# Reordering the opening of an FFT-attention and ELU-MLP kernel: what is asked for first, who prepares the bias and M3, and in which order M2 is made

## The chip, the cores and the metric

One core of one Trainium2 chip. The metric is the device time of one execution in microseconds (us), the median of several runs. The engines are named as in the profile: PE (TensorE; PEld is its weight load), DVE (VectorE), ACT (ScalarE), POOL (GpSimd) and SP (SyncE, which here only issues DMAs).

## The reference, cut to what matters

```python
def _attn_ref(x, w_r, w_i, b_r, b_i):            # x: (8, 3008, 256)
    X = np.fft.rfft(x, axis=1)
    Xr, Xi = X.real, X.imag
    Yr = Xr @ w_r - Xi @ w_i + b_r
    Yi = Xr @ w_i + Xi @ w_r + b_i
    lam = 0.01                                   # soft threshold
    Yr = np.sign(Yr) * np.maximum(np.abs(Yr) - lam, 0.0)
    Yi = np.sign(Yi) * np.maximum(np.abs(Yi) - lam, 0.0)
    return np.fft.irfft(Yr + 1j * Yi, n=3008, axis=1)

def _moe_ref(x, w_in, w_out):                    # x: (24064, 256), d_ff 2048
    h = x @ w_in
    g = np.where(h > 0.0, h, np.exp(np.minimum(h, 0.0)) - 1.0)
    return g @ w_out
```

## The kernel before, in words

The transform of length 3008 = 47 x 64 is done as two steps of matrix products, forward and back. Each of the 8 batches passes five kinds of unit:

- A (6 units a batch, `unit_A`): a product of x with the matrix M1; the result goes from PSUM to the tile A and from there to DRAM (DA). `load_Z` reads it back in another order as Z, in four quarters for batch 0.
- X (8 units, `unit_X`): products of Z with M2, whose 32 slots are used four by four in a unit; two units share a quarter of Z. The result is copied to XT. For batch 0 PSUM has two buffers for A and X (pool `pre2`), so a unit waits for the copy of the one two before it.
- M (12 units): the product with w_r and w_i, bias, and the soft threshold, giving Y. In batch 0 it is `first_M`; there every second unit has the bias added by PE, as a product of a tile of ones (`busy`) with `bias_p`, and its clip is on ACT, while for the other units DVE adds `bias_bc` and POOL clips and subtracts.
- B (6 units, `unit_B`): products of Y with M3, to DRAM (DB) and back as Bs (`load_Bs`).
- Y (8 units): products of Bs with M4, giving yT, the input of the MLP.

The MLP is a long loop over blocks of 512 rows, in which the units of the later batches are woven by a planner; it starts when batch 0 has come through all five. Everything ahead of the loop is the opening. It runs in the order in which the code is written: each engine works through its own instructions in that order and waits where it needs another's result. PE gets filler products (`idle_pe(n)`: n products of `busy` with itself, used by nothing) where it would stand idle.

In the opening the matrices M1 to M4 are computed on the chip from index patterns that POOL makes (`iota`). M2 is made in four groups of slots (g = 0 to 3), each in the passes

- `points(g)` (DVE, three instructions): the phase's integer part, and a sign row `st`;
- `phases(g)` (DVE, or ACT with `on_act`): to turns, in `v2`;
- `wraps(g)` (DVE, two instructions): less the nearest integer;
- `sizes(g)` (ACT): the absolute value, in `a2`; `signs(g)` (DVE): back to a signed phase of the cosine;
- `sines(g, 0)` and `sines(g, 1)` (ACT): the two sines, into M2; `slot0` (DVE, four narrow instructions) mends slot 0.

M3 needs v3 (a product of two index rows), w3 (v3 less its nearest integer, two instructions) and a3 (ACT, the absolute value of w3), then two sines on ACT (`M3f[0]`) and two products on DVE (`M3f[1]`). In the kernel before, DVE makes v3 (L672) behind M2's last signs and w3 (L725, L726) behind it, and a3 stands on ACT (L732) behind the first X copies.

The bias for PE is split into three bf16 parts whose sum is the f32 bias. Before, it comes in three f32 rows (partitions 0, 32 and 64 of `brow`, six DMAs on SP at the very start), is cast on ACT (L727), and DVE takes the rest, casts it, and takes the rest again (L728, L733 to L736).

The DMAs that matter are on two queues, in the order in which they are issued. SP: the bias rows, A's six writes, the weights w_r and w_i (L631, L632), Z's quarters (these wait for all of A's writes), `bias_bc`, the first quarter of w_in, and later B's writes and Bs. POOL: x of batch 0 in six pieces (`first_x`, between the iotas), and, behind a `gate` (L706, a copy that reads one column of Z), x of batch 1 and w_out. POOL also makes `wcat_r` and `wcat_s`, the bf16 weights of M (L633 to L636), and issuing a DMA takes its time.

## Time and profile before

| | before |
| --- | --- |
| runs | 881.12 us median of 3 (880.57 to 881.66) |
| the profiled execution | 879.84 us |
| its span (first to last instruction) | 877.9 us |
| busy share of the span | PE 98%, PEld 80%, ACT 83%, DVE 75%, POOL 74% |
| granted clock of PE | 0.998 |
| x of batch 0: DMAs on POOL's queue | 6 of 512 KB, 6.0 us to landing (median) |
| weights w_r, w_i: DMAs on SP's queue | 2 of 256 KB |

How to read it: times in the profile count from the span's start. The opening is the first 57 us or so. A line of the timeline gives start, length, engine, source line, operation, what is written and read, and in brackets how long the engine stood idle before it and what ended that. A line of the chain of waits gives start, length and what the end of the program hung on at that time. A group (line, engine, operation, tiles, shapes) ends in its count, its busy time, the mean length of one in ns, and its engine's idle time just ahead of it. SPq and POOLq are the DMA issues of SP and POOL.

### The profile page before, as it was taken

Reading aid. Unit: us, or ns where it says so; the run is one execution under the profiler, and the core shown is the slowest. Engines: PE = TensorE matmul, PEld = TensorE weight load, DVE = VectorE, ACT = ScalarE, POOL = GpSimd, SP = SyncE. Lnnn points to the kernel's source line nnn. Section 1 sums busy time; section 2 is a strip of 40 time slices with the busy share of each in tenths; the row PEclk is TensorE's granted clock in tenths of the full one; section 3 lists DMA queues with packets and bytes.
Section 4 is the critical chain, followed back from the end, with each engine's and each line's share of the span. In section 5 each row is a group of like instructions: output and inputs, shape, how many; then the busy total and the mean of one; then the engine's idle time right before and its main releaser. Section 6 shows DMA issues by size and latency. Waiting matters only on the chain.

```text
span 877.9 us, 20548 instructions
## 1 busy us (share of the span) xinstructions
PE 863.4 (98%) x7817; PEld 702.8 (80%) x7817; DVE 656.6 (75%) x1066; ACT 725.9 (83%) x1217; POOL 651.9 (74%) x981
## 2 busy tenths in 40 slices
PE   8889999999999999999999999999999999999997
PEld 3448887888888888888889888898888988888886
DVE  8767886678777787677776777767776788777775
ACT  6668998899888997899978999789987888786664
POOL 6707995689667887698866888668886699756664
PEclk9999999999999999999999999999999999999999
DMA  8995346743484444642564344553444023421111
GB/s 265 354 263 137 113 115 179 203 140 85 127 252 151 124 118 118 180 141 81 151 174 130 125 130 115 154 169 94 137 118 134 26 67 82 129 77 34 43 32 49
DMA packets 106382, 116.68 MB, mean 133 GB/s; under 512 B 10886, under 2 KB 96012, under 8 KB 103404
## 3 DMA queue, kind: packets, MB, share of 16 engines
q1 hardware_dynamic: 100124, 87.85, 35.6%
q0 software_dynamic: 6016, 27.40, 9.9%
q8 instruction: 61, 1.00, 0.5%
q14 instruction: 37, 0.30, 0.1%
q10 hardware_dynamic: 144, 0.13, 0.0%
HBM read 55.32 MB, written 49.81 MB: 120 GB/s over the span
## 4 chain that ended last, share of the span: by engine, by line
PE 86%; POOL 6%; DVE 4%; DMA 1%; issue 1%; ACT 1%; POOLq 0%; DVEq 0%; SPq 0%
PE ps_o L913 36%; PE hps L861 35%; PE mps L262 5%; PE xps L197 2%; PE aps L163 2%; PE yps L397 2%; POOL Et L883 2%; PE bps L356 1%; POOL Y L293 1%; PE mps L214 1%; DVE gT L895 1%; DVE yb L279 1%; POOL yb L288 1%; PE bps L347 1%; POOL clip L289 1%
## 5 line engine op out<-in xcount | busy, mean ns | idle before, releaser
L895 DVE SCALAR_TENSOR_TENSOR gT<-Et,hps 128x512 fp32r<-128x512 f32 x752 | 493.4, 684 | 161.1 <-POOL Et L883 160.2
L913 PE MATMUL ps_o<-w_out_r,gT 128*128 128x256 f32 x3008 | 473.0, 299 | 0.1
L883 POOL TENSOR_SCALAR Et<-Et 128x512 f32<-128x512 f32 x576 | 350.2, 615 | 164.6 <-ACT Et L878 163.4
L861 PE MATMUL hps<-yT,w_in_s 128*128 128x64 bf16 (+9 forms) x2800 | 441.1, 282 | 1.7 <-DVE gT L895 0.6
L913 PEld LDWEIGHTS ps_o<-w_out_r,gT 128*128 128x128 f32 x3008 | 399.4, 188 | 46.3 <-ACT osb L928 0.4
L878 ACT ACTIVATE Et<-hps 128x512 f32<-128x512 f32 x584 | 343.4, 604 | 96.8 <-PE hps L861 93.4
L861 PEld LDWEIGHTS <-w_in_s 128*128 128x128 bf16 x2800 | 163.8, 98 | 57.6 <-issue 13.7
L875 ACT ACTIVATE Et<-hps 128x512 f32<-128x512 f32 x168 | 99.6, 593 | 18.8 <-PE hps L861 18.0
L876 ACT ACTIVATE Et<-Et 128x512 f32<-128x512 f32 x168 | 106.2, 632 | 5.3
L293 POOL TENSOR_TENSOR Y<-yb,clip 128x512 bf16<-128x512 f32 x84 | 108.6, 1293 | 0.3
L288 POOL TENSOR_TENSOR yb<-yb,bias_d 128x256 f32<-128x256 f32 x68 | 49.8, 732 | 29.8 <-DVE yb L279 29.6
L289 POOL TENSOR_SCALAR clip<-yb 128x512 f32<-128x512 f32 x84 | 51.6, 614 | 13.2 <-DVE yb L275 7.0
L246 POOL TENSOR_TENSOR Xd<-XT 128x256 bf16<-128x256 bf16 x84 | 56.5, 673 | 0.0
L130 ACT CAST A<-aps 128x1024 bf16<-128x1024 f32 x45 | 45.3, 1009 | 6.9 <-PE aps L163 6.8
L130 ACT CAST XT<-xps 128x768 bf16<-128x768 f32 x61 | 48.5, 794 | 3.0 <-PE xps L197 3.0
L130 ACT CAST yT<-yps 128x752 bf16<-128x752 f32 x63 | 49.2, 781 | 2.1 <-PE yps L397 2.1
L262 PE MATMUL mps<-wsum,XT 128*128 128x256 bf16 x336 | 50.4, 273 | 0.0
L279 DVE TENSOR_TENSOR yb<-mps,Kb 128x512 f32<-128x512 f32 x68 | 47.0, 692 | 2.5
L278 DVE TENSOR_TENSOR Kb<-mps,bias_bc 128x256 f32<-128x256 f32 x68 | 28.7, 422 | 23.3 <-PE mps L262 23.3
L163 PE MATMUL aps<-xt,M 128*128 128x512 f32 x96 | 38.0, 477 | 2.1 <-DMA xt<-in_x_dram 0.9
L397 PEld LDWEIGHTS <-Bs 96*128 96x128 bf16 x512 | 27.8, 98 | 13.3 <-DMA Bs<-DB 1.8
L370 ACT CAST Bz<-bps 128x1024 bf16<-128x1024 f32 x36 | 36.3, 1007 | 0.0
(124 smaller groups left out, 503.8 us busy)
## 6 DMA issues: line engine op xcount, KB each, us to landing
xt<-in_x_dram POOLq DMA_DIRECT2D x21, 1024.0 KB, 5.6
out_dram<-osb SPq DMA_DIRECT2D x158, 128.0 KB
Bs<-DB SPq DMA_DIRECT2D x32, 384.0 KB
DA<-A SPq DMA_DIRECT2D x21, 512.0 KB
DB<-Bz SPq DMA_DIRECT2D x20, 512.0 KB
Z<-DA SPq DMA_DIRECT2D x26, 384.0 KB
Yt<-Y SPq DMA_DIRECT2D x144, 64.0 KB
xt<-in_x_dram POOLq DMA_DIRECT2D x6, 512.0 KB, 6.0
```

What stands on the lines that cost most here:

```text
L130: nc.scalar.copy(dst, src)
L262: nc.tensor.matmul(dst, lhsT=lhs(dt), rhs=rhs(dt), start=dt == 0, stop=dt == 1)
L288: nc.gpsimd.tensor_tensor(yb[:, D : 2 * D], yb[:, D : 2 * D], bias_d[:], ALU.add)
L289: nc.gpsimd.tensor_scalar(clips[0][:], yb[:], LAM, -LAM, ALU.min, ALU.max)
L293: nc.gpsimd.tensor_tensor(Y_, two(yb), two(clips[0]), ALU.subtract)
L861: nc.tensor.matmul(hps[s][:, a:z], lhsT=w_in_s[:, dt, ft * P : ft * P + P], rhs=yT_of[b][:, dt, t0 + a - c0 : t0 + z - c0], start=(dt == 0 ...
L875: nc.scalar.activation(e, h, AF.Relu, scale=-1.0)
L876: nc.scalar.activation(e, e, AF.Exp, scale=-1.0)
L878: nc.scalar.activation(e, h, AF.Exp)
L883: nc.gpsimd.tensor_scalar(e, e, 1.0, 0.0, ALU.min, ALU.max)
L895: nc.vector.scalar_tensor_tensor(g_of[self.i][:, p], self.E[:, p], -1.0, self.h[p], ALU.add, ALU.max)
L913: nc.tensor.matmul(po[q][:, i_ % 2, :], lhsT=gT[:, s, i_ * P : i_ * P + P], rhs=w_out_r[:, ft, :], start=(ft == 0 and i_ % 2 == 0), stop=( ...
```

## The change

What is asked for first: w_r and w_i are the first two DMAs of SP, ahead of everything; the bias comes in two DMAs of 4 x 64 in place of six of 1 x 256. On POOL's queue `first_x(0)` moves ahead of the first iota. Fillers at the start: 7 in place of 9.

The bias: POOL splits it, on 8 partitions x 64 elements (five narrow instructions), into `bpart`; DVE clears `bias_p`, and three DMAs on SP, behind Z's, put the parts into rows 0 to 2. DVE's and ACT's six instructions on the bias go.

M3's phases: v3 and w3 go from DVE to POOL (four instructions with the scaled index row n2s), w3's last one behind the first request for x of batch 1; a3 moves on ACT from behind unit 1 to behind unit 6 of X.

The weights of M: `wcat_r` goes from POOL to ACT (two copies, among the sines), `wcat_s` stays on POOL, behind w3's first instruction.

M2's passes: DVE makes group 1's phases at once, groups 2 and 3 have theirs on ACT, and the sines of groups 0 and 1 stand next to each other; `slot0` and groups 2 and 3 follow. Fillers ahead of X: 31 in place of 40.

Copies: unit 5 of A uses two PSUM buffers of the M units' pool, and its halves are copied by DVE and ACT at once (`both`). X's units are copied by ACT and DVE in turn (before, DVE had units 1, 4 and 7). The gate reads Z's first quarter (slot 0), not its second (slot 8).

```diff
-    def unit_A(b, u, alone=False, on_dve=False, ahead=False):
+    def unit_A(b, u, alone=False, on_dve=False, ahead=False, both=False):
...
-        ps = unit_ps("aps", alone or ahead)
+        if both:
+            two = [pre1.tile([P, 512], F32, name="aps", tag="mps1")[:] for _ in range(2)]
+        else:
+            ps = unit_ps("aps", alone or ahead)
+            two = [ps[:, j, :] for j in range(2)]
...
+            if both:
+                for j in range(2):
+                    evac(dst[:, 512 * j : 512 * j + 512], two[j], j == 0)
+            else:
+                evac(dst, ps[:].rearrange("p a b -> p (a b)"), on_dve)
...
-    brow, rest = (wk3.tile([P, 2 * D], F32, name="yb", tag="yb") for _ in range(2))
-    nc.vector.memset(brow[:], 0.0)
-    for o, bv in ((0, b_r), (D, b_i)):
-        for k in range(3):
-            nc.sync.dma_start(
-                brow[32 * k : 32 * k + 1, o : o + D],
-                bass.AP(tensor=bv.tensor, offset=bv.offset, ap=[[0, 1], [1, D]]),
-            )
-    idle_pe(9)
+    brow_t = wk3.tile([P, 2 * D], F32, name="yb", tag="yb")
+    bpart_t = wk3.tile([P, 4 * D], BF16, name="yb", tag="yb")
+    brow = brow_t[0:8, 0 : 2 * N2].rearrange("p (k d) -> p k d", k=2)
+    bpart = bpart_t[0:8, 0 : 3 * N2].rearrange("p (k d) -> p k d", k=3)
+    w_r_f, w_i_f = (wk3.tile([P, 2, D], F32, name=nm, tag="Y") for nm in ("w_r_f", "w_i_f"))
+    nc.sync.dma_start(w_r_f[:], w_r.rearrange("(c p) e -> p c e", p=P))
+    nc.sync.dma_start(w_i_f[:], w_i.rearrange("(c p) e -> p c e", p=P))
+    for o, bv in ((0, b_r), (4, b_i)):
+        nc.sync.dma_start(
+            brow[o : o + 4, 0], bass.AP(tensor=bv.tensor, offset=bv.offset, ap=[[N2, 4], [1, N2]])
+        )
+    idle_pe(7)
...
+        first_x(0)
         pcol = iota("pcol", [P, 1], [[0, 1]], cm=1)
...
-        first_x(0)
         first_x(1)
...
+        nc.vector.memset(bias_p, 0.0)
...
+        for k in range(3):
+            pool.tensor_copy(bpart[:, k], brow[:, k % 2])
+            if k < 2:
+                pool.tensor_tensor(brow[:, 1 - k], brow[:, k], bpart[:, k], ALU.subtract)
...
-            unit_A(0, u, alone=True)
+            unit_A(0, u, alone=True, both=u == 5)
...
         points(1)
-        phases(1, True)
+        phases(1)
+        wraps(1)
+        sizes(0)
         points(2)
-        sizes(0)
         fA(4)
-        wraps(1)
-        signs(0)
+        sizes(1)
         fA(5)
-        nc.sync.dma_start(w_r_f[:], w_r.rearrange("(c p) e -> p c e", p=P))
-        nc.sync.dma_start(w_i_f[:], w_i.rearrange("(c p) e -> p c e", p=P))
-        pool.tensor_copy(wcat_r[:, :, 0:D], w_r_f[:])
-        pool.tensor_copy(wcat_r[:, :, D : 2 * D], w_i_f[:])
-        pool.tensor_scalar(wcat_s[:, :, 0:D], w_i_f[:], -1.0, None, ALU.mult)
-        pool.tensor_copy(wcat_s[:, :, D : 2 * D], w_r_f[:])
         for g in range(4):
             load_Z(0, 8 * g, 8 * g + 8)
+        for k in range(3):
+            nc.sync.dma_start(
+                bias_p[k : k + 1, :].rearrange("p (a d) -> p a d", a=8), bpart[:, k]
+            )
...
+        phases(2, True)
         sines(0, 0)
-        sizes(1)
-        phases(2, True)
+        sines(1, 0)
+        signs(0)
+        sines(0, 1)
...
+        full = [P, NV, N2]
+        n2s = row("n2s", [P, N2])
+        pool.tensor_scalar(n2s[:], n2row, 1.0 / S, None, ALU.mult)
+        pool.tensor_tensor(
+            v3[:], n2s[:].unsqueeze(1).to_broadcast(full), k3[:].unsqueeze(2).to_broadcast(full),
+            ALU.mult,
+        )
+        pool.tensor_scalar(w3[:], v3[:], CMAGIC, -CMAGIC, ALU.add, ALU.add)
+        pool.tensor_scalar(wcat_s[:, :, 0:D], w_i_f[:], -1.0, None, ALU.mult)
+        pool.tensor_copy(wcat_s[:, :, D : 2 * D], w_r_f[:])
+        signs(1)
+        nc.scalar.copy(wcat_r[:, :, 0:D], w_r_f[:])
+        nc.scalar.copy(wcat_r[:, :, D : 2 * D], w_i_f[:])
+        sines(1, 1)
+        slot0()
+        wraps(2)
+        sizes(2)
         points(3)
-        phases(3)
-        wraps(2)
-        signs(1)
-        sines(0, 1)
-        sines(1, 0)
-        sizes(2)
-        sines(1, 1)
+        phases(3, True)
+        signs(2)
+        sines(2, 0)
+        sines(2, 1)
         wraps(3)
-        signs(2)
-        slot0()
-        sines(2, 0)
         sizes(3)
-        sines(2, 1)
         signs(3)
...
-        dve.scalar_tensor_tensor(
-            v3[:], n2row.unsqueeze(1).to_broadcast(full), 1.0 / S, k3b, ALU.mult, ALU.mult
-        )
-        idle_pe(40)
+        idle_pe(31)
...
-    gate(Z_of[0][:, 8, 0:1])
-    for ci in range(3):
-        load_x(1, ci)
+    gate(Z_of[0][:, 0, 0:1])
+    load_x(1, 0)
+    nc.gpsimd.tensor_tensor(w3[:], v3[:], w3[:], ALU.subtract)
+    load_x(1, 1)
+    load_x(1, 2)
...
-    nc.vector.tensor_scalar(w3[:], v3[:], CMAGIC, -CMAGIC, ALU.add, ALU.add)
-    nc.vector.tensor_tensor(w3[:], v3[:], w3[:], ALU.subtract)
-    nc.scalar.copy(bias_p, brow[:])
-    nc.vector.tensor_tensor(rest[:], brow[:], bias_p, ALU.subtract)
     for u in range(8):
-        unit_X(0, u, alone=True, on_dve=u in (1, 4, 7))
-        if u == 1:
+        unit_X(0, u, alone=True, on_dve=bool(u % 2))
+        if u == 6:
             nc.scalar.activation(a3[:], w3[:], AF.Abs)
-            nc.vector.tensor_copy(bias_p[32:64], rest[32:64])
-            nc.vector.tensor_copy(bias_p[64:P], rest[64:P])
-            nc.vector.tensor_tensor(rest[64:P], rest[64:P], bias_p[64:P], ALU.subtract)
-            nc.vector.tensor_copy(bias_p[64:P], rest[64:P])
```

More of the change, by code (lines that the diff above doesn't have):

```diff
@@ L160, in unit_A @@
         dav = DA_of[b].rearrange("j p d -> p j d")
-        ps = unit_ps("aps", alone or ahead)
+        if both:
[3 more added lines that the diff above has]
+            two = [ps[:, j, :] for j in range(2)]
         for j in range(2):
             nc.tensor.matmul(
-                ps[:, j, :], lhsT=M1[:],
+                two[j], lhsT=M1[:],
                 rhs=xt[:, 4 * uu + 2 * j : 4 * uu + 2 * j + 2, :], start=True, stop=True,
@@ L167, in done @@
         def done():
-            evac(
-                A[:, 4 * uu : 4 * uu + 4, :].rearrange("p n d -> p (n d)"),
-                ps[:].rearrange("p a b -> p (a b)"), on_dve,
-            )
+            dst = A[:, 4 * uu : 4 * uu + 4, :].rearrange("p n d -> p (n d)")
+            if both:
[3 more added lines that the diff above has]
+                evac(dst, ps[:].rearrange("p a b -> p (a b)"), on_dve)
             j0 = 8 * ci
@@ L462 @@
         w3, a3 = (wk2.tile([P, NV, N2], F32, name="A", tag="A") for _ in range(2))
-        w_r_f, w_i_f = (wk3.tile([P, 2, D], F32, name=nm, tag="Y") for nm in ("w_r_f", "w_i_f"))
         nc.scalar.activation(dume[:], busy[:, 0:1], AF.Sin, bias=0.0, scale=0.0)
+        first_x(0)
         pcol = iota("pcol", [P, 1], [[0, 1]], cm=1)
@@ L667 @@
         sines(3, 1)
-        full = [P, NV, N2]
-        k3b = k3[:].unsqueeze(2).to_broadcast(full)
-        dve.scalar_tensor_tensor(
-            v3[:], n2row.unsqueeze(1).to_broadcast(full), 1.0 / S, k3b, ALU.mult, ALU.mult
-        )
-        idle_pe(40)
+        idle_pe(31)
     gatep = ctx.enter_context(tc.tile_pool(name="gatep", bufs=2))
```

## The prediction

> **What bounds the kernel now.** Read first: the span and the busy shares, then busy time by stretches of the opening (columns: length, busy time and instructions of PE, PEld, DVE, ACT, POOL, granted clock, DMA share, GB/s).
>
> ```profile
> span 877.9 us, 20548 instructions
> PE 863.4 (98%) x7817; PEld 702.8 (80%) x7817; DVE 656.6 (75%) x1066; ACT 725.9 (83%) x1217; POOL 651.9 (74%) x981
> 13.40:22.90 9.50, 9.35 (x42) 4.12 (x42) 9.15 (x23) 8.01 (x16) 4.28 (x5) 1.00 0.91 262
> 22.90:31.04 8.14, 5.69 (x74) 3.55 (x74) 7.31 (x11) 5.50 (x8) 6.16 (x8) 1.00 1.05 326
> 31.04:47.30 16.26, 16.26 (x106) 6.96 (x106) 9.78 (x14) 11.69 (x16) 10.81 (x12) 1.00 1.29 353
> ```
>
> TensorE is busy to 98% of the span, so a microsecond that the opening saves ahead of the first M unit goes through to the end, if what follows comes along. From 31.04 to 47.30 PE never rests. In the 9.5 us before 22.9 most of PE's work is fillers. So the part that can shrink is what lies ahead of 31.04. The chain of waits there (start, length, what):
>
> ```profile
> 20.96 0.52 DVE a L581
> 21.47 0.88 DVE Bz L672
> 22.38 0.86 DVE A L725
> ...
> 24.13 1.10 DVE yb L728
> 25.23 0.88 DVE XT L128
> ...
> 30.02 0.97 DVE XT L128
> ...
> 48.73 3.03 DMA DB<-A
> ```
>
> VectorE carries it: after its share of M2 it computes M3's phases (L672, L725, L726) and the split of the bias (L728), and only then empties X's unit 1, at 25.23. Its last X copy ends at 30.99; call this T. The other leg of the opening is data, seen in the timeline and the DMA issues:
>
> ```profile
> 0.83 0.14 POOL L451 IOTA pcol<- 128x1 f32 x1 [0.40 <-POOLq L1137]
> 1.48 1.36 POOL L119 DMA_DIRECT2D xt<-in_x_dram  x2
> 6.15 0.71 POOL L119 DMA_DIRECT2D xt<-in_x_dram  x1
> 7.62 8.04 SPq L175 DMA_DIRECT2D DA<-A  x6
> xt<-in_x_dram POOLq DMA_DIRECT2D x1, 512.0 KB, 7.2
> 13.38 1.90 ACT L130 CAST A<-aps 128x1024 bf16<-128x1024 f32 x2
> 18.78 1.27 SPq L186 DMA_DIRECT2D Z<-DA  x3
> 22.91 0.37 PEld L197 LDWEIGHTS <-Z 96*128 96x128 bf16 x8 [0.61 <-DMA Z<-DA]
> 24.44 0.37 PEld L197 LDWEIGHTS <-Z 96*128 96x128 bf16 x8 [0.56 <-DMA Z<-DA]
> ```
>
> The last x piece is asked for at 6.15 and lands 7.2 later, 13.35. Its A unit is copied by 15.28 (13.38 + 1.90), Z is asked for at 18.78, and Z's quarters land at 22.9 and 24.4, so by the same step of 1.53 (my estimate for the last two) at 26.0 and 27.5.
>
> **The change part by part.**
>
> *Weights and x asked for first.* x's first request moves ahead of three iotas and two memsets, 0.65 earlier (1.48 to 0.83). One request takes half of 1.36, so the iotas end where they ended, about when VectorE is free to use them. Ahead of x, SP asks for 0.52 MB of weights as soon as the engines start (about when pcol does, 0.83); it had asked for them behind A's writes. What this costs x is read from the queues (packets, MB), up to 3 (one row, x alone) and from 9 to 12, and from the rates of three stretches:
>
> ```profile
> q0 software_dynamic: 5, 0.02, 3.7%
> ...
> q0 software_dynamic: 289, 1.05, 105.3%
> q1 hardware_dynamic: 38, 0.02, 2.7%
> 3.00:4.00 1.00, 1.00 (x4) 0.32 (x3) 0.89 (x5) 0.23 (x1) 1.00 (x5) 1.00 0.83 157
> 4.00:5.00 1.00, 0.96 (x4) 0.23 (x2) 0.79 (x6) 0.03 (x1) 0.93 (x5) 1.00 1.09 389
> 18.00:19.00 1.00, 1.00 (x7) 0.43 (x5) 0.96 (x4) 0.99 (x3) 0.00 (x0) 1.00 0.96 326
> ```
>
> A's writes (q1) were asked for from 7.6 on and got 38 packets in these 3 us beside x's 289: requests are served nearly in the order in which they come. So the weights go before most of x. At 326 GB/s they take 1.6 us; they can start about 1 us before x did (x had 5 packets by 3, its first full microsecond is 3 to 4), and the slow first microsecond (157 against 389 GB/s) falls to them. x's last piece lands 0.5 later, 13.85, by my estimate. Bounds: 0.65 earlier (weights wholly in the idle start) and 0.95 later (1.6 less 0.65). The two bias requests behind them are 1 KB each, and one request a bias replaces three.
>
> [...]
>
> *Unit 5's copy split over both engines.* ACT did units 4 and 5 in one row of 1.90. Now unit 5 is two halves at once; a 512-wide ACT copy is the 602 ns row below. 13.85 + 0.70 (matmuls) + 0.6 = 15.15: 0.1 earlier than 15.28 (bounds -1.25 and +0.35, those of x).
>
> *No weights behind A's last write.* From the last write's issue (right behind the copy, about 15.3; SP's six end at 15.66) to Z's request pass 3.4 us, with the weights' packets in the same queue; the write in the chain's row, DB<-A, took 3.03. I take 0.6 off (bounds 0 and 0.9). Z's request is then 0.7 earlier, 18.1; Z's quarters land at 22.2, 23.7, 25.3, 26.8.
>
> *M2's passes.* The last sine was:
>
> ```profile
> 21.50 0.52 ACT L591 ACTIVATE M<-a 96x384 bf16<-96x384 f32 x1 [0.93 <-DVE a L581]
> L727 ACT CAST spare<-yb 128x512 bf16<-128x512 f32 x1 | 0.6, 602 | 0.0
> L130 ACT CAST XT<-xps 128x768 bf16<-128x768 f32 x5 | 4.0, 797 | 3.0 <-PE xps L197 3.0
> ```
>
> It ended at 22.0. The work is the same, but ACT gains two copies of the weights (2 x 0.60) among it, and phase 1 goes from ACT to VectorE while phase 3 goes the other way. ACT waited 0.93 for VectorE before this sine, so part of the copies hides in such waits. I take 22.9 for ACT's last sine and 22.4 for VectorE's last sign; bounds 22.0 (all hidden) and 23.9 (both copies and 0.7 of contention on the path). ACT's copies of X queue behind that sine.
>
> *X.* VectorE now has nothing between its signs and X's copies, and copies alternate. Two PSUM buffers take turns; a unit's matmuls take 0.5, a copy 0.8 on ACT and 0.95 on VectorE (30.02's row: 0.97):
>
> ```profile
> 22.91 0.52 PE L197 MATMUL xps<-M,Z 96*128 96x96 bf16 x8
> 19.39 3.40 PE L412 MATMUL ips<-spare 128*128 128x512 bf16 x15
> ```
>
> ACT copies unit 0 from 22.95 to 23.75; unit 2's matmuls run 23.8 to 24.3, its copy to 25.15; unit 4 waits for Z at 25.3, copy 25.9 to 26.7; unit 6 waits for Z at 26.8, copy 27.4 to 28.2. VectorE: unit 1 23.35 to 24.3, unit 3 24.9 to 25.85, unit 5 26.45 to 27.4, unit 7 (matmuls 27.45 to 27.95) 28.0 to 28.95. T = 28.95 against 30.99: **2.0 earlier**. The fillers ahead of X, 31 instead of 40 at 0.22 (3.40 by 15), end at 14.55 + 6.9 = 21.4 and stay off the path; 40 would end at 23.4 and cost 1.2.
>
> *M3 and the bias.* VectorE loses L672, L725, L726 and L728 to L736, about 6 us in all; GpSimd gets M3's phases and the bias parts. ACT's Abs, which stood after unit 1, now follows unit 6, and the two sines of M3 behind it. The rows that tell what waits:
>
> ```profile
> 31.04 0.96 DVE L747 SCALAR_TENSOR_TENSOR M3f<-M3f,sg 128x768 bf16<-128x768 bf16 x1
> 32.69 1.25 POOL L328 TENSOR_SCALAR clip<-yb 128x512 f32<-128x512 f32 x1 [3.63 <-DVE yb L224]
> 34.02 1.27 POOL L329 TENSOR_TENSOR Y<-yb,clip 128x512 bf16<-128x512 f32 x1
> 35.68 0.61 PE L347 MATMUL bps<-Y,M3f 64*128 64x256 bf16 x8
> ```
>
> L747 needs M3's first sine: 28.2 + 0.75 (Abs) + 0.75 = 29.7, 0.75 after unit 7's copy where it began 0.05 after it. The first bias add behind it on VectorE, then GpSimd's clip and subtraction (34.02 + 1.27 = 35.29, T + 4.3), come 0.55 later against T, at T + 4.85; PE's first B unit came at T + 4.7. Queued behind Abs on ACT, which now waits for GpSimd's w3, are both sines and the clips of every second M unit. So **0.15 is lost again** (bounds 0 and 1).
>
> *GpSimd.* It sat idle for 5.14 us up to 19.33 (first row). Now it has the bias parts (five narrow operations, about 2 us by estimate; the 512-wide L633 took 0.75), v3 and w3 (768 wide), wcat_s, the gate, one x request, w3's subtraction, then the other requests. Prices:
>
> ```profile
> 19.33 0.75 POOL L633 CAST wcat_r<-w_r_f 128x512 bf16<-128x512 f32 x1 [5.14 <-DMA w_r_f<-in_w_r_dram]
> L329 POOL TENSOR_TENSOR Y<-yb,clip 128x512 bf16<-128x512 f32 x5 | 6.3, 1269 | 0.4
> L289 POOL TENSOR_SCALAR clip<-yb 128x512 f32<-128x512 f32 x84 | 51.6, 614 | 13.2 <-DVE yb L275 7.0
> L635 POOL TENSOR_SCALAR wcat_s<-w_i_f 128x512 bf16<-128x512 f32 x1 | 3.1, 3091 | 0.0
> ```
>
> At L329's and L289's rates: v3 1.9, w3 0.9, wcat_s 1.2, gate and request 1.3, subtraction 1.9: 14.2 + 2 + 0.3 for n2's row + 7.2 = 23.7. But L635, the same work as L289, took 3.09 while VectorE ran L581 and L672. Half of that delay on 3.4 us of work until VectorE falls free gives about 27.5, still before ACT wants w3 at 28.2; the weight requests behind end near 31, before the first clip. It costs nothing, with little to spare.
>
> [...]
>
> The gate now asks for Z's first quarter, not its second, but stands behind wcat_s in the queue; all of Z is requested by then and, in the order of service above, x(1) doesn't take its place. The three bias parts on SP's queue are small and follow Z. After M nothing changes, and x(1) and w_out are asked for at about the old times.
>
> **Sum.** -2.0 + 0.15 = -1.85. The profiled execution took 879.84 (877.9 is its span), 1.28 under the median of the runs, 881.12; it becomes 878.0, and the median 879.3. Range of this case: 878.6 (last sine at 22.0, Z 1.0 earlier, nothing lost in M, T = 28.5) to 880.5 (last sine at 23.9, Z as before, T = 30.0, 0.4 lost).
>
> **Rivals.** (1) *The weights cost x nothing*: they are over before x starts. For it: DMA moves nothing before 2.9. x's last piece lands at 12.7, Z at 21.4, M2 ends at 22.4; X is then bound by the copies, T = 28.45, -2.4: 878.7. (2) *The weights push x back in full*, and A's tail gains nothing: x +0.95, Z's request +0.35, last quarter 27.85; unit 7 is copied by 30.0, -1.0 + 0.15: 880.3. For it: the order of service above. (3) *GpSimd becomes the bound* (slower): at L635's rate v3 and w3 take 4.6 each, wcat_s 4.1, so w3's subtraction ends at about 33. From w3 to the first B unit lie Abs, sine, L747, bias add, clip, subtraction, 5.9 us, so PE's first B unit waits from w3 = 29.8 on; the old time is passed at that point, and 33 gives +3.2, 884.3; between a bare loss and that, 883.5. [...]
>
> **How the numbers follow.** What a measurement of this kernel can tell from no change is about 0.2%, 1.76 us: faster is under 879.36, slower over 882.88. Forecast 0.50 (0.28 faster, 0.22 same); rival 1 0.20, faster; rival 2 0.15, same; rival 3 0.15 (0.12 slower, 0.03 same). Faster 0.48, same 0.40, slower 0.12. The range runs from 877.7 (rival 1 with X bound by Z alone and all 0.9 of A's tail won, T = 27.6) to 882.0 (into rival 3).
>
> **What would show it.** Right: Z's request near 18.1, the first XT copy on ACT near 23.0 right behind the last sine, T near 29, the first B unit near 33.8, GpSimd's w3 done by 28. Wrong: x's last piece later than 14.3; w3 later than 29.8 with PE idle ahead of the first B unit; or the DB<-A and Bs<-DB steps longer than before, so that the gain is given back behind M.

## The result, and the profile after

The changed kernel takes 883.93 us (median of 20 runs, 881.50 to 885.64), the kernel before on the same chip 880.93 (20 runs). The ratio is 1.003, 95% interval 1.0022 to 1.0038: slower by 0.3%, where 0.2% faster was forecast. The profiled execution is the longest of the 20 (885.64, span 883.4), so its delays are some 1.7 above those of a median run. The profile of the kernel before is of a quick execution (879.84), so the two profiles lie further apart than the two medians.

The page of the changed kernel, span and busy times:

```profile
span 883.4 us, 20404 instructions
PE 864.5 (98%) x7689; PEld 705.1 (80%) x7806; DVE 654.5 (74%) x1060; ACT 725.5 (82%) x1217; POOL 657.3 (74%) x988
```

The shares are those of before; an average over 880 us doesn't show what happened in the first 60. Next, TensorE's timeline of the changed kernel (start, length, what; in brackets how long it had been idle and who ended that):

```profile
1.45 3.17 PE L418 MATMUL ips<-spare 128*128 128x512 bf16 x7 [1.45 <-DVE spare L412]
7.25 1.19 PE L167 MATMUL aps<-xt,M 128*128 128x512 f32 x2 [2.63 <-DMA xt<-in_x_dram]
8.24 1.50 PE L418 MATMUL ips<-spare 128*128 128x512 bf16 x3
...
24.67 0.51 PE L203 MATMUL xps<-M,Z 96*128 96x96 bf16 x8
28.57 0.80 PE L203 MATMUL xps<-M,Z 96*128 96x96 bf16 x8 [3.17 <-ACT XT L130]
29.59 0.84 PE L203 MATMUL xps<-M,Z 96*128 96x96 bf16 x8
...
40.34 0.61 PE L353 MATMUL bps<-Y,M3f 64*128 64x256 bf16 x8 [0.20 <-POOL Y L335]
```

Two rests of 2.63 and 3.17 stand out, and behind each TensorE is slow. Three fillers between A's units take 1.50; in the kernel before they took 0.82:

```profile
6.39 0.82 PE L412 MATMUL ips<-spare 128*128 128x512 bf16 x3
```

But in A the slow rate isn't shown to come from the rest: the seven fillers ahead of it already take 3.17, the last two of them 1.06 where the last two of the kernel before take 0.59. The first fillers of the kernel before are as slow (three in 1.46); there, nine of them precede A, and A's rows are at the full rate. In X the rate was full ahead of the rest and slow behind it: a unit takes 0.84 instead of 0.51. X's units then come 1.06 apart and TensorE itself paces them. The windows around the second rest (columns as in the prediction; the granted clock is the third number from the end):

```profile
24.10:28.57 4.47, 1.30 (x19) 0.95 (x20) 3.42 (x6) 3.37 (x7) 1.04 (x4) 0.83 0.95 237
28.57:34.20 5.63, 5.41 (x52) 4.23 (x53) 1.92 (x2) 2.13 (x3) 5.32 (x6) 0.53 0.93 276
```

TensorE runs at 0.53 of its clock for 5.63 us. Why it rested there is seen on the other engines: unit 2 waits for a copy on ACT, which stands behind M2's last sine. The last rows of ACT's M2 and the first X copy, and VectorE's and GpSimd's timelines beside them:

```profile
27.31 0.52 ACT L600 ACTIVATE M<-a 96x384 bf16<-96x384 f32 x1 [0.27 <-DVE a L590]
27.74 0.78 ACT L130 CAST XT<-xps 128x768 bf16<-128x768 f32 x1
...
16.91 0.60 DVE L590 SCALAR_TENSOR_TENSOR a<-a,c,st 96x384 f32<-96x384 f32 x1
17.99 1.92 DVE L590 SCALAR_TENSOR_TENSOR a<-a,c,st 96x384 f32<-96x384 f32 x1
21.81 0.96 DVE L555 TENSOR_SCALAR mi<-mi 96x384 int32<-96x384 int32 x1
22.81 0.84 DVE L556 SCALAR_TENSOR_TENSOR kv<-mi,kk 96x384 f32<-96x384 int32 x1
24.26 0.95 DVE L590 SCALAR_TENSOR_TENSOR a<-a,c,st 96x384 f32<-96x384 f32 x1
...
18.02 1.47 POOL L668 TENSOR_TENSOR Bz<-n2s,k 128x768 f32<-128x768 f32 x1 [1.57 <-DVE k L663]
19.58 2.99 POOL L672 TENSOR_SCALAR A<-Bz 128x768 f32<-128x768 f32 x1
22.54 1.59 POOL L673 TENSOR_SCALAR wcat_s<-w_i_f 128x512 bf16<-128x512 f32 x1
24.08 0.72 POOL L674 CAST wcat_s<-w_r_f 128x512 bf16<-128x512 f32 x1
```

The same L590 takes 0.60 while GpSimd does nothing wide, and 1.92 beside GpSimd's L668; L555 and L556 take 0.96 and 0.84, where e7 below, with GpSimd idle, has 0.35 and 0.56. The last sine ends at 27.83, forecast 22.9, before 22.02. X's last copy ends at 35.36 (T; before 30.99), the first B unit begins at T + 4.98.

Where the loss arises is seen from a milestone further on: the first M row past 80 us begins at 88.39 before and at 93.80 after (5.41 between these two executions, 3.0 between the medians), and from it to the end of the span pass 789.5 and 789.6. In every profile below whose trace is used that distance lies between 788.9 and 789.9. So everything is decided in the first 90 us.

The execution of e1 that was profiled took 2,263.61 us against 881.95 to 883.73 in its ten others, so its trace isn't used.

### The profile page after: what moved, and what is told of

Read it like the earlier page. It is cut to its first block, busy times and chain, and to the rows that moved or that the text cites. A ratio compares the mean times of both kernels' runs of the same rounds, so it can differ in the third digit from the quotient of the medians.

```text
span 883.4 us, 20404 instructions
## 1 busy us (share of the span) xinstructions
PE 864.5 (98%) x7689; PEld 705.1 (80%) x7806; DVE 654.5 (74%) x1060; ACT 725.5 (82%) x1217; POOL 657.3 (74%) x988
## 4 chain that ended last, share of the span: by engine, by line
PE 85%; POOL 6%; DVE 4%; DMA 3%; issue 1%; ACT 1%; POOLq 0%; SPq 0%; DVEq 0%
PE ps_o L924 37%; PE hps L872 32%; PE mps L268 5%; PE aps L167 3%; PE xps L203 3%; POOL Et L894 2%; PE yps L403 2%; PE bps L362 1%; POOL Y L299 1%; DMA Z<-DA 1%; DVE gT L906 1%; PE ips L418 1%; DVE yb L285 1%; POOL yb L294 1%; DMA DA<-A 1%
## 5 line engine op out<-in xcount | busy, mean ns | idle before, releaser
L872 PE MATMUL hps<-yT,w_in_s 128*128 128x512 bf16 (+8 forms) x2688 | 416.9, 278 | 1.8 <-DVE gT L906 0.6
L130 ACT CAST A<-aps 128x1024 bf16<-128x1024 f32 (+1 forms) x45 | 45.0, 999 | 9.7 <-PE aps L167 9.4
L167 PE MATMUL aps<-xt,M 128*128 128x512 f32 x96 | 40.3, 502 | 2.9 <-DMA xt<-in_x_dram 2.6
L203 PEld LDWEIGHTS <-Z 96*128 96x128 bf16 x512 | 29.1, 101 | 13.5 <-issue 4.3
L203 PE MATMUL xps<-M,Z 96*128 96x96 bf16 x512 | 34.0, 212 | 4.8 <-ACT XT L130 3.2
```

The lines of the kernel that those rows point to most:

```text
L130: nc.scalar.copy(dst, src)
L167: nc.tensor.matmul(two[j], lhsT=M1[:], rhs=xt[:, 4 * uu + 2 * j : 4 * uu + 2 * j + 2, :], start=True, stop=True,)
L203: nc.tensor.matmul(psv[:, kk, 0 : 4 * K1], lhsT=Z[:, k, dt * P : dt * P + P], rhs=M2[:, k].rearrange("p c m -> p (c m)"), start=True, stop ...
L872: nc.tensor.matmul(hps[s][:, a:z], lhsT=w_in_s[:, dt, ft * P : ft * P + P], rhs=yT_of[b][:, dt, t0 + a - c0 : t0 + z - c0], start=(dt == 0 ...
```

## The experiments

Milestones of all profiles (us from the span's start; "product" is the first row of the output layer's product ps_o), and the ratio to the kernel before over all runs:

| kernel | last sine ends | T | first B | first Y | product | ratio, 95% interval |
|---|---|---|---|---|---|---|
| before | 22.02 | 30.99 | 35.68 | 55.97 | 61.47 | |
| after | 27.83 | 35.36 | 40.34 | 60.75 | 66.25 | 1.003 (1.0022 to 1.0038) |
| e1 | | | | | | 1.0022 (1.0012 to 1.0031) |
| e2 | 25.95 | 31.84 | 36.66 | 56.98 | 63.39 | 1.0021 (1.0009 to 1.0032) |
| e3 | 23.85 | 30.58 | 35.28 | 56.20 | 62.75 | 1.0006 (0.9996 to 1.0016) |
| e5 | 25.63 | 32.44 | 37.16 | 57.46 | 63.20 | 1.0025 (1.0015 to 1.0034) |
| e6 | 25.79 | 33.97 | 38.67 | 58.88 | 65.53 | 1.0032 (1.0022 to 1.0042) |
| e7 | 22.39 | 29.33 | 34.02 | 55.53 | 63.23 | 0.9999 (0.9988 to 1.001) |
| e8 | 25.77 | 31.66 | 36.49 | 56.79 | 62.29 | 1.0005 (0.9995 to 1.0015) |
| e9 | 23.71 | 30.24 | 34.93 | 55.65 | 61.39 | 0.9979 (0.9965 to 0.9994) |
| e10 | 22.70 | 29.83 | 34.52 | 55.69 | 62.32 | 0.9988 (0.9978 to 0.9998) |
| e11 | 22.63 | 29.29 | 33.98 | 54.90 | 61.53 | 0.9989 (0.998 to 0.9999) |
| e12 | 21.93 | 30.89 | 35.58 | 55.74 | 61.25 | 0.9998 (0.9986 to 1.0009) |
| e13 | 27.34 | 34.82 | 39.84 | 60.13 | 65.63 | 1.0025 (1.0012 to 1.0039) |
| e14 | 23.12 | 30.55 | 35.24 | 56.03 | 61.76 | 0.9993 (0.9981 to 1.0005) |
| e15 | 21.92 | 30.89 | 35.58 | 56.35 | 61.85 | 1.0007 (0.9996 to 1.0018) |

Each profile is one execution, and two of kernels that are alike up to Y differ: T is 29.29 in e11 and 30.55 in e14. Below, the time of a kernel is its median; the kernel before, run beside each group on the same chip, had medians of 880.80 to 881.14.

**e1: TensorE kept busy at the start.**

```
-    idle_pe(7)
+    idle_pe(16)
```

> Sixteen fillers on TensorE at the start in place of seven, so that it does not idle for 2.63 us ahead of A. Clock theory (TensorE runs slower after an idle stretch, and that slower TensorE paces A): the fillers between A's units fall from 1.50 for three to about 0.8, a pair of A's matmuls from 1.2-1.4 to 0.70, the last A unit begins at 13.8-14.2 instead of 15.68, and Z is asked for near 18.4 instead of 20.03. Theory that GpSimd's work slows VectorE's passes of M2: the last sine still ends at 27.0 or later whatever A does, so the end of X (T, 35.36 in the changed kernel) falls by less than 1, and the time stays at 883 to 884. If the slow start alone were the cause of the loss, T would be about 33 and the time 881.5.

882.92, 1.0 under the changed kernel, with overlapping intervals, and just under the 883 to 884 of the theory of GpSimd's work. The milestones can't be read. It says no more than that the slow start is not the whole: that would have given 881.5.

**e2: TensorE kept busy in X's rest.**

```
-        idle_pe(1)
+        idle_pe(13 if u == 1 else 1)
```

> Thirteen fillers between X's units 1 and 2 in place of one; they cover the 3.17 us in which TensorE idled there. Clock theory: X's units 2 to 7 then run at 0.5 a unit instead of 0.84, the copies bind them, T is 32.5 (31.9 to 33.1) instead of 35.36, and the time is about 881.5. Rival: X is bound by its copies and not by TensorE: T stays within 0.4 of 35.4 and the time at 884. The last sine is not touched and ends near 27.8 in both.

TensorE's rows of this kernel:

```profile
23.18 2.97 PE L418 MATMUL ips<-spare 128*128 128x512 bf16 x13
26.68 1.06 PE L203 MATMUL xps<-M,Z 96*128 96x96 bf16 x16 [0.54 <-ACT XT L130]
28.07 0.50 PE L203 MATMUL xps<-M,Z 96*128 96x96 bf16 x8
...
58.36 2.45 PE L872 MATMUL hps<-yT,w_in_s 128*128 128x512 bf16 x12 [0.54 <-ACT yT L130]
```

X's units are back at 0.50 and T at 31.84: the slow rate, not the copies, had paced X. From the last sine to T pass 5.9, after the change 7.5. The last sine, which should have stayed near 27.8, came at 25.95 in this execution, whose A was slow for a shorter time; so 1.9 of the 3.5 that T moved isn't the fillers' doing. But the time is 883.47, hardly less; 881.5 was expected. The last row shows one reason: the input layer (hps, thirteen matmuls in 1.75 in the changed kernel's profile) is slow here, twelve in 2.45, behind another rest of 0.54; the granted clock from 56.00 to 63.00 is 0.76. A third place for the same loss lies behind M.

**e3: M3's phases back on VectorE, behind its last sign.**

```
-        pool.tensor_tensor(
-            v3[:], n2s[:].unsqueeze(1).to_broadcast(full), k3[:].unsqueeze(2).to_broadcast(full),
-            ALU.mult,
-        )
-        pool.tensor_scalar(w3[:], v3[:], CMAGIC, -CMAGIC, ALU.add, ALU.add)
...
         sines(3, 1)
+        dve.scalar_tensor_tensor(
+            v3[:], n2row.unsqueeze(1).to_broadcast(full), 1.0 / S,
+            k3[:].unsqueeze(2).to_broadcast(full), ALU.mult, ALU.mult,
+        )
...
-    nc.gpsimd.tensor_tensor(w3[:], v3[:], w3[:], ALU.subtract)
...
+    nc.vector.tensor_scalar(w3[:], v3[:], CMAGIC, -CMAGIC, ALU.add, ALU.add)
+    nc.vector.tensor_tensor(w3[:], v3[:], w3[:], ALU.subtract)
```

> M3's phases (v3, w3, w3's subtraction) back on VectorE behind its last sign; GpSimd keeps wcat_s, the bias parts and the requests. Theory that GpSimd's wide work slows VectorE: L590's and L555's rows go back to 0.61 and 0.35 wherever wcat_s does not run beside them, the last sine ends near 25.2 instead of 27.8, TensorE's gap ahead of unit 2 shrinks to about 1 us, and T is 31 to 32.5, the time 880.5 to 882. Rival, that M2 is late because A (behind the cold TensorE) holds its engines: the last sine stays at 27 or later, and with 2.7 us more on VectorE T is 36 or more and the time 884.5 or more.

The last sine ends at 23.85, T at 30.58, and the time is 881.51: 2.4 of the loss of 3.0 is gone, with 2.5 us of work more on VectorE ahead of X's unit 1. The rival (T at 36) falls. But moving the phases also takes the chain to M3's sines off GpSimd, and e6 separates that.

**e5: the weights asked for behind A's last write, as before the change.**

```
-    nc.sync.dma_start(w_r_f[:], w_r.rearrange("(c p) e -> p c e", p=P))
-    nc.sync.dma_start(w_i_f[:], w_i.rearrange("(c p) e -> p c e", p=P))
...
         fA(5)
+        nc.sync.dma_start(w_r_f[:], w_r.rearrange("(c p) e -> p c e", p=P))
+        nc.sync.dma_start(w_i_f[:], w_i.rearrange("(c p) e -> p c e", p=P))
```

> The weights' two requests behind A's last write again, as before the change. Theory that the weights ahead of x cost x's first piece: the first A unit begins near 6.0 instead of 7.25, TensorE's gap ahead of it is 1.4 instead of 2.63, x's last piece lands 0.4 to 1.0 earlier, and the last A unit begins 1 to 2 us earlier if TensorE keeps its clock; Z is asked for near 19. T, if the last sine is VectorE's and GpSimd's matter, changes by less than 1, and the time is 883 to 884. Rival (weights are free, x is late for GpSimd's own late first request): the first A unit stays at 7.0 or later.

The first A unit begins at 5.47, after a rest of 0.85, so the rival isn't borne out, as far as one execution tells; the time, 882.96, can't be told from the changed kernel's (the intervals overlap). TensorE's first A unit in e5, and what the late weights do to ACT in M2:

```profile
5.47 1.19 PE L167 MATMUL aps<-xt,M 128*128 128x512 f32 x2 [0.85 <-DVE c L444]
...
19.09 0.62 ACT L676 CAST wcat_r<-w_r_f 128x512 bf16<-128x512 f32 x1 [1.94 <-DMA w_r_f<-in_w_r_dram]
```

ACT now waits 1.94 for the weights, so part of what x wins is lost there, and T, 32.44, stays bound to a late sine (25.63). T was to move by less than 1 and moved by 2.9; as in e2, A was slow for a shorter time than in the changed kernel's profile. How early A begins also scatters: with the weights first and seven fillers it is 5.91, 5.95, 6.83, 7.05, 7.16 and 7.25 (e3, e7, e13, e2, e6, after). With this scatter one profile can't price the order of the requests at the start (by unit 5 it is 0.5 on the mean, below); it isn't what made the loss.

**e6: GpSimd's wide work without anything that hangs on it.** e3, and GpSimd computes M3's two wide passes once more, into a3, which ACT's Abs later overwrites:

```
+        pool.tensor_tensor(
+            a3[:], n2s[:].unsqueeze(1).to_broadcast(full), k3[:].unsqueeze(2).to_broadcast(full),
+            ALU.mult,
+        )
+        pool.tensor_scalar(a3[:], a3[:], CMAGIC, -CMAGIC, ALU.add, ALU.add)
         pool.tensor_scalar(wcat_s[:, :, 0:D], w_i_f[:], -1.0, None, ALU.mult)
```

> As e3_m3_dve (M3's phases on VectorE), and GpSimd does the two wide operations of M3's phases once more, into a buffer that nobody reads until ACT's Abs overwrites it: GpSimd's load beside M2 is that of the changed kernel, while no result hangs on it. Theory that GpSimd's work beside M2 slows VectorE: VectorE's rows beside it go up to 0.8-1.9 again, the last sine ends 1.5 to 3 later than in e3_m3_dve (23.85 there), that is at 25.4 to 27, and the time rises by 1.5 to 2.5 to about 883.5. Rival, that the loss came from the chain v3, w3, Abs, sines hanging on GpSimd, or from the order of VectorE's passes: the last sine stays within 0.5 of 23.85 and the time at 881.5.

884.0, 2.5 over e3: the whole loss is back, although no result of the repeated passes is used. VectorE's and GpSimd's timelines of e6:

```profile
17.00 2.50 DVE L609 TENSOR_SCALAR M<-M,c 96x24 bf16<-96x24 bf16 x4
...
21.51 0.96 DVE L590 SCALAR_TENSOR_TENSOR a<-a,c,st 96x384 f32<-96x384 f32 x1
22.40 0.76 DVE L585 TENSOR_SCALAR r<-v 96x384 f32<-96x384 f32 x1
...
16.88 1.53 POOL L668 TENSOR_TENSOR A<-n2s,k 128x768 f32<-128x768 f32 x1
18.50 2.80 POOL L672 TENSOR_SCALAR A<-A 128x768 f32<-128x768 f32 x1
21.26 1.68 POOL L673 TENSOR_SCALAR wcat_s<-w_i_f 128x512 bf16<-128x512 f32 x1
```

Both sides lose, in turns. Four scalings of M (L609) take 2.50 beside L668 and the first 1.0 of L672; L672 takes 2.80, while VectorE's rows beside the rest of it keep their lengths (L585 0.34, L586 0.56, L555 0.35, L556 0.56, as in e3, where GpSimd is idle beside them); and beside wcat_s VectorE's L590 and L585 are slow again (0.96 for 0.61, 0.76 for 0.35). The last sine ends at 25.79, 1.9 after e3's; T is 3.4 later, since TensorE rests 2.90 in X and from the next unit on is slow (the granted clock is 0.72 from 24 to 31). The passes also push wcat_s back, but M doesn't wait for it: from T to the first B unit pass 4.70 in e3 and in e6.

**e7: GpSimd does nothing wide beside M2.** e3, with wcat_s behind the x requests:

```
-        pool.tensor_scalar(wcat_s[:, :, 0:D], w_i_f[:], -1.0, None, ALU.mult)
-        pool.tensor_copy(wcat_s[:, :, D : 2 * D], w_r_f[:])
...
     load_x(1, 2)
+    nc.gpsimd.tensor_scalar(wcat_s[:, :, 0:D], w_i_f[:], -1.0, None, ALU.mult)
+    nc.gpsimd.tensor_copy(wcat_s[:, :, D : 2 * D], w_r_f[:])
```

> As e3_m3_dve, with wcat_s on GpSimd behind batch 1's x requests, so that GpSimd does nothing wide beside M2. Theory that GpSimd slows VectorE: the last scaling of M (L609, 1.10 for four there, and k3's 0.76) goes down to about 0.6, the last sine ends 0.3 to 0.8 before 23.85; wcat_s is ready by 29.5, ahead of M's first unit. Time 0 to 0.8 under e3_m3_dve's 881.5. Rival, that what remains is the order of the passes between VectorE and ACT: the last sine stays at 23.6 to 24.

VectorE's and ACT's timelines, and TensorE behind M, of e7:

```profile
16.48 0.68 DVE L609 TENSOR_SCALAR M<-M,c 96x24 bf16<-96x24 bf16 x4
...
19.17 0.61 DVE L590 SCALAR_TENSOR_TENSOR a<-a,c,st 96x384 f32<-96x384 f32 x1
...
21.87 0.52 ACT L600 ACTIVATE M<-a 96x384 bf16<-96x384 f32 x1 [0.27 <-DVE a L590]
...
28.37 0.96 DVE L128 CAST XT<-xps 128x768 bf16<-128x768 f32 x1 [0.59 <-PE xps L203]
...
57.73 2.74 PE L870 MATMUL hps<-yT,w_in_s 128*128 128x512 bf16 x13 [1.04 <-DVE yT L128]
```

L609 takes 0.68 (2.50 in e6), the last sine ends at 21.87 + 0.52 = 22.39 and T is 29.33, close to the prediction's 22.9 and 28.95 although VectorE does M3's phases. The time, 880.64, is that of before: of the 1.66 that T won, the profile shows nothing left at the product (63.23 against 61.47). From the first B unit to Y pass 21.51, before 20.29, and from Y to the product 7.70, before 5.50, at a granted clock of 0.56.

**e8: all three rests covered, GpSimd's work left in place.**

```
-    idle_pe(7)
+    idle_pe(11)
...
-        idle_pe(1)
+        idle_pe(13 if u == 1 else 1)
...
-    idle_pe(3)
+    idle_pe(9)
     for u in range(2):
         unit_Y(0, u, alone=True, on_dve=bool(u % 2))
```

> The changed kernel with fillers in all three gaps of TensorE: 11 at the start for 7, 13 behind X's unit 1 for 1, 9 ahead of Y for 3; GpSimd's work stays. Clock theory: no row of PE in the first 90 us shows the slower rate (fillers 0.27 each, X's unit 0.50), and the time falls from 883.9 by what the slow rate costs, which I put at 1.5 on the mean, to 882.4; the runs lie closer together (under 2 between lowest and highest). The theory that GpSimd's work is the main loss leaves T near 32 in it, 1 behind the kernel before, and the time 1.5 over before. If the clock were the whole loss, the time would be 881.

The windows of A, of X and from Y to the product in e8:

```profile
5.73:14.84 9.11, 7.47 (x29) 2.93 (x29) 7.80 (x25) 5.74 (x7) 8.07 (x25) 1.00 1.08 345
22.00:31.66 9.66, 8.11 (x85) 4.74 (x85) 6.33 (x8) 6.44 (x11) 7.09 (x9) 1.00 0.97 262
56.79:62.29 5.50, 4.24 (x53) 2.62 (x51) 3.46 (x7) 3.86 (x7) 0.00 (x0) 1.00 1.13 346
```

The clock is full everywhere, T is 31.66 and the time 881.58, 2.3 under the changed kernel; the runs lie within 1.55. That is more than the 1.5 expected of the clock, but not the whole loss: the late sine (25.77) is still there. T is 0.7 behind the kernel before, and so is the time (880.89 beside it); behind e7, whose sine isn't late, T is 2.3. The runs' mean granted clocks agree: 0.9971 to 0.9979 before (four groups of 21 to 35 runs), 0.9947 after (20 runs), 0.9988 in e8 (12). The 0.0024 to 0.0032 between the first two is 2.1 to 2.8 us of an 880 us span.

**e9: both causes removed as far as they were known.** e3 with 11 and 9 fillers, M3's first pass ahead of VectorE's last sign and the two others behind its copy of unit 3.

```
+        dve.scalar_tensor_tensor(
+            v3[:], n2row.unsqueeze(1).to_broadcast(full), 1.0 / S,
+            k3[:].unsqueeze(2).to_broadcast(full), ALU.mult, ALU.mult,
+        )
         signs(3)
...
+        if u == 3:
+            nc.vector.tensor_scalar(w3[:], v3[:], CMAGIC, -CMAGIC, ALU.add, ALU.add)
+            nc.vector.tensor_tensor(w3[:], v3[:], w3[:], ALU.subtract)
```

> M3's phases on VectorE, the first ahead of its last sign and the two others behind its copy of X's unit 3, with 11 fillers at the start and 9 ahead of Y. If the two causes (GpSimd beside M2, the slow rate of TensorE behind its gaps) are the whole of the loss, this one gives what the change can give: X's unit 1 is copied from 24.5 instead of 25.7, T is 29.0 to 29.8, TensorE keeps its rate, and the time is 1 to 2 under before, 879 to 880. If something else is lost behind M, T is as early but the time no better than before.

880.06, ratio 0.9979 (0.9965 to 0.9994): faster than both kernels, by 0.8 than the one before where 1 to 2 were expected, and T (30.24) is later than the 29.0 to 29.8 expected. Its last sine ends at 23.71, with wcat_s still beside M2.

**e10 and e11: e7 and e9 put together.** e10 is e7 with 11 fillers at the start and 9 ahead of Y; e11 also spreads M3's phases as e9 does.

> As e7_ws_late (nothing wide on GpSimd beside M2), with 11 fillers at the start and 9 ahead of Y. In e7_ws_late X ended at 29.33, 1.65 before the kernel before, and M's tail behind it was lost to the slow rate (from the first B unit to the first product of the output layer 29.2, against 25.8 before). Clock theory: the second distance goes back to 25.8, the first product comes at 59.8 instead of 63.2, and the time is 878 to 879, faster than before by 0.2 to 0.3%. Rival, that the gain of X is lost to transfers behind M whatever TensorE's rate: the distance stays at 27 or more and the time at 880.5.

> As e10_ws_late_fill, with M3's phases on VectorE between its passes and its copies (the first ahead of the last sign, two behind unit 3's copy), so that unit 1 is copied sooner. X's copies bind X: T 28.6 to 29.2 and the time 0 to 0.7 under e10_ws_late_fill. Rival: ACT's Abs, which now comes behind these, delays M3's sines, and the first B unit comes no earlier than 34.0: no gain.

880.70 and 880.24: each faster than before by 0.1%, neither by what T promised. The first B units begin 1.2 and 1.7 earlier than before, the products 0.85 later and 0.06 later. TensorE in e10, behind M:

```profile
55.69 0.84 PE L403 MATMUL yps<-M,Bs 96*128 96x94 bf16 x16 [0.74 <-DMA Bs<-DB]
57.57 1.77 PE L870 MATMUL hps<-yT,w_in_s 128*128 128x512 bf16 x11 [1.04 <-DVE yT L128]
59.55 0.63 PE L870 MATMUL hps<-yT,w_in_s 128*128 128x512 bf16 x1 [0.22 <-issue]
```

Nine fillers did not keep the clock: a single matmul takes 0.63, where one takes 0.38 in the changed kernel (64.27), and the granted clock from 58.00 to 61.00 is 0.61. e10's clock theory expected 25.8 from B to the product; 27.8 came, and with 880.70 the numbers of its rival. Both have a part: 0.9 of the 2.0 lies between B and Y, 1.1 between Y and the product, where the rate is slow. In e11 the first B unit (33.98) still comes 4.69 after T, so ACT's later Abs, its rival, held nothing up.

**e12 and e13: the fillers ahead of Y alone**, nine for three, in the kernel before (e12) and in the changed one (e13).

> The kernel before with 9 fillers ahead of Y in place of 3, and nothing else. Its profile shows no slow rate there, so that if that holds for most of its runs the time stays at 880.9 (0.3 either way). Rival: part of its runs fall into the slow rate behind M too; then its median falls by 0.5 or more and its runs lie closer together, and part of what the other kernels win by these fillers isn't the change's.

> The changed kernel with 9 fillers ahead of Y in place of 3, and nothing else. Two looks at related kernels showed the slow rate behind M cost 0.6 to 3.4 there. Clock theory: 0.5 to 1.2 under the changed kernel, 882.7 to 883.4; together with the starts (0.9) and X's gap (0.5) that adds to what all fillers gave (2.3). If it stays at 883.9, the gaps don't add up and the gain of all fillers lies in the two others.

881.09 and 883.88: no difference in either. So e9 does not owe its gain to those fillers alone. One rest alone gave 1.0 (e1), 0.5 (e2) and nothing here, 1.5 together, where all at once gave 2.3. Each of these is known to about 0.9 only, so whether they add up isn't settled.

**e14 and e15: the rests behind M covered wholly**, in e11 (12 fillers ahead of Y) and in the kernel before (9):

```
     for u in range(2):
         unit_Y(0, u, alone=True, on_dve=bool(u % 2))
+    idle_pe(4)
```

> As e11_ws_late_mid (X ends at 29.29 there, the first B unit at 33.98), with 12 fillers ahead of Y for 9 and 4 more behind Y's first two units, so that TensorE rests less than 0.7 at a time behind M. Clock theory: from the first row of Y to the first product of the output layer 5.5 again (6.63 in e11), and 1.0 less time than e11, about 879.3. Transfer theory: from the first B unit to the first row of Y stays at 20.9 (20.29 before), since the last write of B, 4.00 there for 3.03, still shares the queues; that 0.6 stays lost.

> The kernel before with the same fillers behind M (9 ahead of Y for 3, 4 behind Y's first units), as a control: time unchanged within 0.5 of 880.9, since its profile shows no slow rate there. If it falls by 0.5 or more, that part of what e14 wins isn't the change's.

TensorE in e14:

```profile
56.03 0.83 PE L403 MATMUL yps<-M,Bs 96*128 96x94 bf16 x16
56.69 1.03 PE L418 MATMUL ips<-spare 128*128 128x512 bf16 x4
57.90 1.49 PE L872 MATMUL hps<-yT,w_in_s 128*128 128x512 bf16 x13 [0.17 <-DVE yT L128]
...
27.65 0.51 PE L203 MATMUL xps<-M,Z 96*128 96x96 bf16 x8 [0.52 <-DMA Z<-DA]
```

From Y to the product pass 5.73: with the rests covered the granted clock is 1.00 from 55.00 to 64.00, as the clock theory has it. From B to Y pass 20.79 against 20.29 before, as the transfer theory has it. This step also scatters: e15 shows 20.77 and e12, alike up to Y, 20.16. The time, 880.85, is no better than e11's; e15's is 881.55, not to be told from the kernel before. In e14's profile X ended late (T 30.55, with the same code ahead as e11's 29.29) because units 4 and 6 waited for Z: the last quarter was used from 27.65 (the last row above), in e11 from 26.34.

What became of T's gain is seen in three places of the profiles. From B to Y pass 20.7 to 21.5 in the six kernels whose T is 30.6 or earlier, 20.2 to 20.4 in the others but e15. From Y to the product some lose the rate. And from the product to the first M row past 80 us pass 26.9 in before, e3, e7, e10, e11 and e13, but 27.4 to 28.4 in the others. There, in all but the changed kernel, TensorE stands once more, for 0.3 to 0.6 on batch 1's Z (e8, e9, e14, e15) or 0.8 to 1.35 on the input layer's result gT (e2, e5, e6, e12). In e9 the chain of waits goes through batch 1's write of A and its read as Z:

```profile
54.18 7.30 DMA DA<-A
61.60 8.14 DMA Z<-DA
```

e12 and e15, the kernel before with fillers alone, reach that M row 1.0 and 0.9 later than the kernel before does in its profile, which met no such wait. How much each place costs on the mean stays open, with one profile for each kernel.

## Why the prediction was wrong

**x and the weights: right within its bounds.** The request came at 1.27, not 0.83. SP asked for the weights at 0.73. GpSimd's first DMA, now its first work, began 0.44 later than pcol's iota had (0.83), and pcol came at 2.06. Where TensorE kept its rate in A, unit 5's matmuls end at 14.27 to 14.84, 14.50 on the mean (e7 to e11 and e14), and at 13.86 to 14.14, 14.02 on the mean, in the old order (before, e12, e15): 0.5 later, as forecast.

**Unit 5's split and A's tail: right.** Where A was not slow, Z is asked for at 17.93 to 18.48 (the same six), forecast 18.1. In the changed kernel's profile it was asked for at 20.03, as A's matmuls were slow (the first three pairs 1.19, 1.41 and 1.42). No step of the prediction had that: "7 in place of 9" fillers at the start was priced at nothing. With seven, A's first pair is slow (1.19) in five of seven profiles (after, e3, e5, e6, e13) and at the full rate (0.70, 0.71) in e2 and e7; with nine or eleven it is at the full rate in seven of eight and takes 0.96 in e12.

**M2's passes: the step that failed.** The prediction took "22.9 for ACT's last sine", with an upper bound of 23.9 that held "0.7 of contention on the path". It came at 27.83 in the profile, and at 25.6 to 27.3 in every kernel that kept GpSimd's two passes beside M2 (e2, e5, e6, e8, e13). With wcat_s alone beside M2 it comes at 23.85 and 23.71 (e3, e9), without anything wide on GpSimd at 22.39 to 23.12 (e7, e10, e11, e14). So the sum of M2's own work was right, and the contention was mis-sized: no run shows that 0.7, the profiles show about 3, and 1.5 to 2 more in the changed kernel's and e13's profiles, where A was slow. The sum charged the contention to GpSimd ("half of that delay on 3.4 us of work"), since the row that showed it was a GpSimd row, L635 with 3.09. The runs show that VectorE pays as well (L609 0.68 without GpSimd's passes in e7, 2.50 with them in e6), and VectorE's passes were on the path.

**X: right where M2 was.** Forecast T 28.95, bounds 28.5 and 30.0; e7, e10 and e11 have 29.33, 29.83 and 29.29, with M3's phases on VectorE, and e14, where Z came late, 30.55. In the changed kernel two errors met here: the last sine was 4.9 later than forecast, and while TensorE waited for it, it lost its clock (granted 0.53 from 28.57 to 34.20), so that a unit took 0.84 where the sum had 0.5. "The fillers ahead of X ... stay off the path" was right, and beside the point: what mattered was the rate behind the rest within X, which the prediction never priced and which fillers in that rest kept up in e2 and e8 (0.50 a unit). e8 puts the slow rate at 2.3 of the loss of 3.0; e7, without the contention, takes all 3.0 away. The two overlap, since the late sine is what makes the rest in X.

The slow rate is known here by its length and its scatter. The slow stretch in X lasted about 4.9 in the changed kernel (28.57 to the filler at 33.43) and about 3.3 in e5 (26.09 to within the unit at 29.16). e3 and e7 both rested 1.3 ahead of A, and A's first pair took 1.19 in one and 0.71 in the other. In e10 the clock fell behind rests of 0.74 and 1.04.

**M3 and the bias: right in kind.** The first B unit came at T + 4.98, forecast T + 4.85, before T + 4.69.

**GpSimd and rival 3.** w3 was done at 30.95, past 29.8 where the third rival had it decide. But ACT's Abs began only at 34.37 behind its own X copies, so w3 was not waited for:

```profile
27.89 0.19 POOL L723 CAST gate<-Z 96x1 f32<-96x1 bf16 x1 [3.09 <-ACT M L600]
29.09 1.86 POOL L739 TENSOR_TENSOR A<-Bz,A 128x768 f32<-128x768 f32 x1
34.37 0.85 ACT L747 ACTIVATE A<-A 128x768 f32<-128x768 f32 x1
```

The sum had w3 at 27.5, and its working doesn't hold as it is worded: half of L635's delay (2.48 on 0.61 of work) on 3.4 us would be about 6.9, not 3.8. The passes from v3 to wcat_s took 6.8 where the rates give 4.0. What made w3 late besides were two waits that the sum didn't have: v3 stood 1.57 for VectorE's k3, and the gate 3.09, until M2's last sine had ended. The rival's time (883.5) was near the result by luck: its mechanism wasn't what happened. The contention was there (L672 2.99), but what it delayed on the path was the other engine (VectorE's L590 1.92 for 0.60).

**What "After M nothing changes" missed.** The kernel before rests 1.28 and 0.54 behind M and keeps its rate there (granted clock 1.00 from 55.97 to 61.47):

```profile
55.97 0.84 PE L397 MATMUL yps<-M,Bs 96*128 96x94 bf16 x16 [1.28 <-DMA Bs<-DB]
57.35 1.75 PE L861 MATMUL hps<-yT,w_in_s 128*128 128x512 bf16 x13 [0.54 <-ACT yT L130]
```

Six variants lost it there: e3 and e7 behind a longer first rest (1.79 and 2.36), e6, e10 and e11 with a longer second one (1.04), e2 with 1.17 and 0.54. The granted clock is 0.50 in e7 and e11 and 0.61 in e10 (58.00 to 61.00), 0.76 in e2 (56.00 to 63.00) and 0.83 in e3 and e6 (55.00 to 65.00). From Y to the product they take 6.4 to 7.7 instead of 5.5, up to 2.2 more. And the prediction's own last sign of being wrong came true in the variants: B's last write (DB<-A) takes 3.7 to 4.0 in e3, e7, e9, e10 and e11, before 3.03.

## What to carry to other kernels

When a row shows one engine slowed by another, price the delay on both of them, and above all on the one that lies on the path: work moved to the idle GpSimd was not free for VectorE here (four scalings took 2.50 beside it in e6, 0.68 without it in e7). A test that needs no argument is to let the idle engine do the work into a buffer that nobody uses (e6). And where an opening stretches a rest of TensorE, or takes fillers away ahead of its first work, look for a slower rate behind it, not only at the rest: X's units took 0.84 behind a rest of 3.17 in the changed kernel, and 0.50 where thirteen fillers, which look like waste, stood in it (e2, e8).

## What was not expected of the hardware

- Four 96x24 bf16 scalings took 0.68 with GpSimd idle, 1.10 beside wcat_s (e3) and 2.50 beside two 768-wide GpSimd passes (e6). A 768-wide GpSimd pass took 2.80 to 2.99 beside VectorE, where L289's rate (512 wide in 0.61) gives 0.92.
- The longest rest alone didn't decide here whether TensorE lost its clock. Behind rests of 0.74 and 1.04 the granted clock was 0.61 (e10, 58.00 to 61.00), with 1.17 and 0.54 it was 0.76 (e2, 56.00 to 63.00, the rests among them), and with 1.28 and 0.54 it was 1.00 (before, 55.97 to 61.47).
- The granted clock of the windows is 1.00 from 4.62 to 13.00 in the changed kernel, while the matmuls there take nearly twice their time (three fillers 1.50), and 1.00 over the seven slow fillers ahead (1.45 to 4.62). In e2, where the rate fell between A's first pair (0.70) and its second (1.26), it is 0.86 from 0.00 to 12.00. So the slow start of the changed kernel is seen in its rows, and not in that column.
